# Attention scores and products with v in rounds of four 64x64 array quarters, with loads reordered and dense groups mixed

## Chip, cores, metric

One core of a Trainium2 chip runs the whole program. The metric is device time in microseconds (us) of one execution. A profile's span is about 1.8 us shorter than the time of the same execution.

## The reference

Batch 8, 12 heads, 448 tokens, head size 64, then a dense block on 3584 tokens:

```python
scores = (1.0 / np.sqrt(64)) * np.matmul(q, k.transpose(0, 1, 3, 2))
attn = np.maximum(scores, 0.0) ** 2 / 448
x = np.matmul(attn, v)              # heads merged: 3584 x 768
h = x @ w_in                        # 768 x 2048
r = np.maximum(h, 0.0)
out = (r * r) @ w_out               # 2048 x 768, float32
```

Attention is worked off in 24 *units* of four heads (three units a batch). The dense block is worked off in *groups*: an h group (6 matmuls, 128 rows of h for one batch) or an output group (16 matmuls, 128 tokens by 384 columns). Output groups need all 16 h groups of their batch. *g* is the squared relu of h that they read. In the profiles the tiles of h are called hps, those of the outputs ops, score tiles sp (their relu sr, their squares at), and the products with v avt, which are scaled into xt.

## The kernel before

Tokens of k are cut into three chunks of 128 and a tail of 64. q and k are cast to fp16 and transposed by DMA. ACT writes relu to SBUF as fp32, DVE multiplies it by itself. A queue holds the dense matmuls, and pieces of it are put between the attention work of a unit.

```python
s_p = ...tile_pool(name="sps", bufs=2, space=PSUM)     # 2 score buffers of 2 banks
mm_p = ...tile_pool(name="mmps", bufs=4, space=PSUM)   # 4 banks for all else

def relu2(ps, dst, shape, tag, scale):
    r = rel_p.tile(shape, FP32, name=tag, tag=tag)
    nc.scalar.activation(out=r, in_=ps, func=AF.Relu, scale=scale)
    nc.vector.tensor_mul(dst, r, r)

def scores(n, hp, t):              # two matmuls side by side, 64 rows each
    ...
    for j in range(2):
        r = slice(64 * j, 64 * j + 64)
        nc.tensor.matmul(sp[:, j, 0:S], lhsT=kT[r, 3 * hp + t, :], rhs=qT[r, hp, :], ...)
# ... scores_tail: four matmuls in the four 64x64 quarters; av: both forms ...

for n in range(NUN):
    # ... loads of unit n+3 ...
    g = [scores(n, 0, 0), scores(n, 0, 1)]; soft(...); soft(...)
    fill(...)                      # dense matmuls from the queue
    st = scores_tail(n)
    if n > 0:
        av(n - 1)                  # 4 + 12 matmuls, DVE scales the result into xt
    soft(n, "tail", st)
    if u == 0 and n > 0:
        push_h(b - 1)              # 16 h groups, then the output groups they allow
        # ... push_o(...) ...
    fill(...)
    # ... w1 loads at n == 0, w2 loads at n == 1, casts and DMA transposes of unit n+2 ...
    g = [scores(n, 0, 2), scores(n, 1, 0)]; soft(...); soft(...)
    fill(...)
    g = [scores(n, 1, 1), scores(n, 1, 2)]; soft(...); soft(...)
    fill(...)
```

Of the kernel before, what the change touches and what calls it, by code (L numbers as in the profile page):

```python
# [15 lines left out]
def kernel(  # L17
# [9 lines left out]
    nc = tc.nc  # L27
# [8 lines left out]
    QP = 112  # L36
    QJ = S // QP
    NU = 3
    NM = DM // P
    NF = FF // P  # L40
    HALF = DM // 2
    KM = 384
    ST = S - KM

# [7 lines left out]
    in_p = ctx.enter_context(tc.tile_pool(name="inp", bufs=2))  # L52
# [3 lines left out]
    rel_p = ctx.enter_context(tc.tile_pool(name="relp", bufs=2))  # L56
    at_p = ctx.enter_context(tc.tile_pool(name="atp", bufs=11))
    x_p = ctx.enter_context(tc.tile_pool(name="xp", bufs=2))
    g_p = ctx.enter_context(tc.tile_pool(name="gp", bufs=32))
    osb_p = ctx.enter_context(tc.tile_pool(name="osbp", bufs=2))  # L60
# [8 lines left out]

    raw: dict = {}  # L70
    qkt: dict = {}
    vst: dict = {}
    ktt: dict = {}

    def load_q(n, eng):
        b, u = divmod(n, NU)
        qf = raw_p.tile([QP, 4, QJ * D], FP32, name="qf", tag="qf")
        eng.dma_start(
            out=qf, in_=q[b, 4 * u:4 * u + 4].rearrange("h (p j) d -> p h (j d)", j=QJ))
        raw[n, "q"] = qf  # L80

    def load_k(n, eng):
        b, u = divmod(n, NU)
        kf = raw_p.tile([P, 4, 3 * D], FP32, name="kf", tag="kf")
        eng.dma_start(
            out=kf, in_=k[b, 4 * u:4 * u + 4, 0:KM].rearrange("h (p t) d -> p h (t d)", t=3))
        raw[n, "k"] = kf

    def turn_q(n, ops):
        qf = raw.pop((n, "q"))  # L90
        qs = blk_p.tile([QP, 2, QJ, 2 * D], FP16, name="qs", tag="qs")
        for j in range(2):
            ops[j](qs[:, :, :, j * D:(j + 1) * D],  # L93
                   qf.rearrange("p (a j) (t d) -> p a j t d", j=2, d=D)[:, :, j])
        qT = qkt_p.tile([P, 2, S], FP16, name="qT", tag="qT")
        nc.sync.dma_start_transpose(
            out=qT.rearrange("p a (j c) -> p (a j) c", j=QJ),
            in_=qs.rearrange("p a t d -> p (a t d)"))
        qkt[n, "q"] = qT

    def turn_k(n, ops):
        kf = raw.pop((n, "k"))
        ks = blk_p.tile([P, 2, 3, 2 * D], FP16, name="ks", tag="ks")
        for j in range(2):
            ops[j](ks[:, :, :, j * D:(j + 1) * D],  # L105
                   kf.rearrange("p (a j) (t d) -> p a j t d", j=2, d=D)[:, :, j])
        kT = qkt_p.tile([P, 6, P], FP16, name="kT", tag="kT")
        nc.sync.dma_start_transpose(  # L108
            out=kT, in_=ks.rearrange("p a t d -> p (a t d)"))
        qkt[n, "k"] = kT  # L110

    def load_kt(b):
        kt = in_p.tile([ST, H, D], FP16, name="kt", tag="kt")
        nc.gpsimd.dma_start(out=kt, in_=k[b, :, KM:S].rearrange("h p d -> p h d"))
        raw[b, "t"] = kt

    def turn_kt(b):
        kt = raw.pop((b, "t"))
        ktT = in_p.tile([P, NM, ST], FP16, name="ktT", tag="ktT")
        nc.sync.dma_start_transpose(out=ktT, in_=kt.rearrange("p h d -> p (h d)"))  # L120
        ktt[b] = ktT

    def load_v(b, h0, h1):
        if b not in vst:
            vst[b] = (in_p.tile([P, H, 3 * D], FP16, name="vs", tag="vs"),
                      in_p.tile([P, H, D], FP16, name="vt", tag="vt"))
        nc.gpsimd.dma_start(
            out=vst[b][0][:, h0:h1, :],
            in_=v[b, h0:h1, 0:KM].rearrange("h (p t) d -> p h (t d)", t=3))

    def load_vt(b):

        for r in range(2):
            nc.gpsimd.dma_start(
                out=vst[b][1][64 * r:64 * r + 64],
                in_=v[b, :, KM:S].rearrange("h p d -> p h d"))

    pool2 = (nc.gpsimd.tensor_copy, nc.gpsimd.tensor_copy)
    dve2 = (nc.vector.tensor_copy, nc.vector.tensor_copy)
    act2 = (nc.scalar.copy, nc.scalar.copy)  # L140
# [13 lines left out]

    load_q(0, nc.sync)
    load_k(0, nc.scalar)
    load_kt(0)
    load_q(1, nc.sync)
    load_k(1, nc.scalar)
    load_v(0, 0, 4)  # L160
    load_vt(0)
    load_w1(0)
    load_v(0, 4, H)
    turn_q(0, dve2)
    turn_k(0, act2)
    turn_kt(0)
    load_q(2, nc.sync)
    load_k(2, nc.sync)
    turn_q(1, dve2)
    turn_k(1, dve2)  # L170


# [5 lines left out]
    def push(cost, fn):  # L178
        nonlocal queued
        fifo.append((cost, fn))  # L180
        queued += cost

    def run_some(ns):
        nonlocal queued
        while fifo and ns > 0:
            c, fn = fifo.popleft()
            fn()
            queued -= c
            ns -= c
        return ns  # L190

    def relu2(ps, dst, shape, tag, scale):
        r = rel_p.tile(shape, FP32, name=tag, tag=tag)
        nc.scalar.activation(out=r, in_=ps, func=AF.Relu, scale=scale)  # L194
        nc.vector.tensor_mul(dst, r, r)  # L195

    def push_h(b):
# [7 lines left out]
        def step(f, m):  # L205
            def run():
# [6 lines left out]
                if m == NM - 1:  # L213
                    if b % 2 == 0:
                        gt[f] = g_p.tile([P, 2 * S], FP16, name="g", tag="g")
                    relu2(cell[0][:, 0:S], gt[f][:, (b % 2) * S:(b % 2 + 1) * S],
                          [P, S], "hr", 1.0)
            return run

        for f in range(NF):  # L220
            for m in range(NM):
                push(189.0, step(f, m))

    def store(pr, tb, osb):
        c = tb * P
        end = c + P
        while c < end:
            b = 2 * pr + c // S
            cb = c % S
            j, p0 = cb // QP, cb % QP  # L230
            n = min(QP - p0, end - c)
            r = c - tb * P
            nc.sync.dma_start(
                out=out[b * S:(b + 1) * S, :].rearrange(
                    "(p j) d -> p j d", j=QJ)[p0:p0 + n, j, :],
                in_=osb[r:r + n, :],
            )
            c += n

    def push_o(pr, tb):  # L240
# [21 lines left out]
        for hf in range(2):  # L262
            for f in range(NF):
                push(162.5, step(hf, f))
# [4 lines left out]
    def soft(n, key, sp):  # L269
        at = at_p.tile([P, 2, S], FP16, name="at", tag="at")  # L270
        relu2(sp[:, :, 0:S], at, [P, 2, S], "sr", SK)
        ats[n, key] = at

    def scores(n, hp, t):
        qT, kT = qkt[n, "q"], qkt[n, "k"]
        sp = s_p.tile([P, 2, 512], FP32, name="sp", tag="s")
        for j in range(2):
            r = slice(64 * j, 64 * j + 64)
            nc.tensor.matmul(  # L279
                sp[:, j, 0:S], lhsT=kT[r, 3 * hp + t, :],  # L280
                rhs=qT[r, hp, :], start=True, stop=True)
        return sp



    QUADS = ((0, 0, 0), (0, 1, 1), (1, 0, 1), (1, 1, 0))

    def scores_tail(n):
        b, u = divmod(n, NU)
        qT, kt = qkt[n, "q"], ktt[b]  # L290
        sp = s_p.tile([P, 2, 512], FP32, name="sp", tag="s")
        for hp, j, c in QUADS:
            r = slice(64 * j, 64 * j + 64)
            nc.tensor.matmul(  # L294
                sp[64 * c:64 * c + 64, hp, 0:S], lhsT=kt[r, 2 * u + hp, :],
                rhs=qT[r, hp, :], start=True, stop=True)
        return sp

    def av(n):
        b, u = divmod(n, NU)  # L300
        vs, vt = vst[b]
        ap = [mm_p.tile([P, 512], FP32, name="avt", tag="mm") for _ in range(2)]
        for hp, j, c in QUADS:
            r = slice(64 * c, 64 * c + 64)
            nc.tensor.matmul(  # L305
                ap[hp][64 * j:64 * j + 64, 0:S], lhsT=vt[r, 4 * u + 2 * hp + j, :],
                rhs=ats[n, "tail"][r, hp, :],
                start=True, stop=False, skip_group_check=True)
        for hp in range(2):
            for t in range(3):  # L310
                for j in range(2):
                    nc.tensor.matmul(  # L312
                        ap[hp][64 * j:64 * j + 64, 0:S],
                        lhsT=vs[:, 4 * u + 2 * hp + j, t * D:(t + 1) * D],
                        rhs=ats[n, (hp, t)][:, j, :],
                        start=False, stop=(t == 2), skip_group_check=True)
            nc.vector.tensor_scalar(  # L317
                out=xts[b][:, 2 * u + hp, :], in0=ap[hp][:, 0:S],
                scalar1=CX, scalar2=None, op0=ALU.mult)

    NUN = B * NU
    KEEP = 4000.0

    def fill(atoms_left):
        run_some(max(0.0, (queued - KEEP) / atoms_left))

    for n in range(NUN):
        b, u = divmod(n, NU)
        if n + 3 < NUN:
            load_q(n + 3, nc.sync)  # L330
            load_k(n + 3, nc.sync)
# [81 lines left out]
```

## Time and profile before

| | before |
|---|---|
| time, median of 7 runs | 467.2 us (466.2 to 468.6) |
| first score matmul / first dense matmul (hps) / first output matmul (ops) | 19.5 / 76.2 / 102.2 us |
| two batches in the steady part | 99.8 us |
| busy: PE / DVE / ACT | 389 / 300 / 236 us |

The page cuts the span (465.7 us) into 40 slices of 11.6 us; a digit is the busy share in tenths.

```profile
PE   0113157899999999989998999989998999999995
DVE  2152567996699367975787469955995478834500
DMA  9999999903891559706990469227933320021022
```

PE (TensorE) is nearly full from the ninth slice on, and at 0 to 5 tenths in the first six, where the DMA row stands at 9. So there are two regimes: a start of some 75 us held by DMA (loads and DMA transposes), and a long part held by TensorE. The chain of work that ended last says what the start waited for; its columns are start us, us, what. It is cut to the start.

```profile
7.25 12.15 DMA kT<-ks
...
26.71 20.22 DMA qf<-in_q_dram
...
53.52 10.71 DMA kf<-in_k_dram
...
70.09 2.78 DMA ktT<-kt
```

Each of the four long pieces is a DMA: the transpose of unit 0's k takes 12.15 us among the loads of weights, a load of q takes 20.22 us. What PE waited for kT, the transposed k, over the whole span (us in total, times, longest):

```profile
PE sp L279 <- DMA kT<-ks: 45.2, 3, 19.5
```

Here is how the first looks in the timeline of PE (start us, us, engine, line, operation, tiles, count, and in brackets the idle time and its releaser):

```profile
302.66 0.65 PE L248 MATMUL ops<-w_3_100,g 128*128 128x384 f16 x3
304.96 0.34 PE L248 MATMUL ops<-w_3_100,g 128*128 128x384 f16 x1 [1.64 <-DVE g L195]
```

Last, the time of DVE's two products, as min/median/max in ns:

```profile
L195 DVE TENSOR_TENSOR at<-sr x168: 1075/1085/2957, 21.0 to 415.0; 128x896 f16<-128x896 f32 x168
L195 DVE TENSOR_TENSOR g<-hr x128: 609/624/1926, 78.9 to 440.5; 128x448 f16<-128x448 f32 x128
```

The medians are 1.2 and 1.4 ns for each element of a partition.

### The profile page before, as it was taken

The numbers are of one execution on the slowest core, as the hardware profiler recorded it, in microseconds if no ns is written. First come the engines' busy times: TensorE is split into PE (matmuls) and PEld (weight loads), VectorE is DVE, ScalarE is ACT, GpSimd is POOL, SyncE is SP. The second block draws the span as 40 slices with busy tenths as digits, with TensorE's granted clock in tenths as the row PEclk, the third lists the DMA queues.
The fourth block names the chain that finished last, engine by engine and source line by source line (L and its number), as shares of the span: only waits on it lengthen the run. The fifth ranks groups of instructions, "written<-read, shape, count | busy, mean of one in ns | idle before, by whom it ended". The sixth has DMA issues, their size and how long they took to land.

```text
span 465.7 us, 6359 instructions
## 1 busy us (share of the span) xinstructions
PE 388.9 (84%) x2432; PEld 185.2 (40%) x2432; DVE 299.7 (64%) x350; ACT 236.4 (51%) x355; POOL 108.2 (23%) x133
## 2 busy tenths in 40 slices
PE   0113157899999999989998999989998999999995
PEld 0001013444444444444444544444444444455563
DVE  2152567996699367975787469955995478834500
ACT  1232354575565457556565456735654567543421
POOL 6050528510442005500432043402440000000000
PEclk9999656999999999999999999999999999999999
DMA  9999999903891559706990469227933320021022
GB/s 208 199 216 218 206 225 220 211 2 80 159 240 39 81 140 175 157 1 156 156 207 1 114 152 220 65 63 163 203 91 71 90 59 1 1 68 35 0 69 68
DMA packets 109614, 56.25 MB, mean 121 GB/s; under 512 B 77840, under 2 KB 106000, under 8 KB 109584
## 3 DMA queue, kind: packets, MB, share of 16 engines
q1 hardware_dynamic: 72032, 41.69, 40.2%
q0 software_dynamic: 36496, 13.37, 24.6%
q10 hardware_dynamic: 1056, 0.79, 0.6%
q8 instruction: 19, 0.31, 0.3%
q14 instruction: 11, 0.09, 0.1%
HBM read 47.19 MB, written 11.01 MB: 125 GB/s over the span
## 4 chain that ended last, share of the span: by engine, by line
PE 51%; DVE 24%; DMA 11%; ACT 8%; SPq 2%; issue 2%; POOL 1%; ACTq 0%; POOLq 0%
PE ops L248 29%; DVE at L195 15%; PE hps L209 12%; DVE g L195 8%; ACT sr L194 6%; DMA qf<-in_q_dram 5%; PE avt L312 5%; PE sp L279 4%; DMA kT<-ks 3%; DMA kf<-in_k_dram 2%; ACT hr L194 2%; SPq L108 1%; PE sp L294 1%; DVE xt L317 1%; PE avt L305 1%
## 5 line engine op out<-in xcount | busy, mean ns | idle before, releaser
L195 DVE TENSOR_TENSOR at<-sr 128x896 f16<-128x896 f32 x168 | 186.7, 1147 | 102.0 <-ACT sr L194 101.5
L194 ACT ACTIVATE sr<-sp 128x896 f32<-128x896 f32 x168 | 147.0, 918 | 91.3 <-PE sp L279 75.8
L248 PEld LDWEIGHTS <-g 128*128 128x128 f16 x896 | 84.0, 98 | 77.6 <-issue 13.9
L194 ACT ACTIVATE hr<-hps 128x448 f32<-128x448 f32 x128 | 68.5, 553 | 60.3 <-DVE g L195 31.9
L195 DVE TENSOR_TENSOR g<-hr 128x448 f16<-128x448 f32 x128 | 89.8, 731 | 13.8 <-ACT hr L194 12.1
L93 POOL CAST qs<-qf 112x512 f16<-112x512 f32 x44 | 41.0, 958 | 231.3 <-DMA qf<-in_q_dram 229.7
L279 PE MATMUL sp<-qT,kT 64*128 64x448 f16 x288 | 44.1, 377 | 52.8 <-DMA kT<-ks 45.2
L255 ACT ACTIVATE osb<-ops 128x384 f32<-128x384 f32 x56 | 27.5, 492 | 69.0 <-PE ops L248 68.9
L248 PE MATMUL ops<-w_3_100,g 128*128 128x384 f16 x224 | 47.7, 327 | 8.6 <-DVE g L195 8.6
L248 PE MATMUL ops<-w_0_97,g 128*128 128x384 f16 x224 | 47.1, 326 | 0.0
L248 PE MATMUL ops<-w_2_99,g 128*128 128x384 f16 x224 | 46.4, 327 | 0.0
L248 PE MATMUL ops<-w_1_98,g 128*128 128x384 f16 x224 | 46.3, 326 | 0.0
L279 PEld LDWEIGHTS <-kT 64*128 64x128 f16 x288 | 9.4, 95 | 81.2 <-DMA kT<-ks 46.4
L317 DVE TENSOR_SCALAR xt<-avt 128x448 f16<-128x448 f32 x48 | 28.2, 618 | 18.9 <-PE avt L312 18.9
L209 PE MATMUL hps<-xt,w_3_96 128*128 128x448 f16 x192 | 40.0, 353 | 0.0
L209 PE MATMUL hps<-xt,w_0_93 128*128 128x448 f16 x192 | 39.6, 358 | 0.0
L209 PE MATMUL hps<-xt,w_1_94 128*128 128x448 f16 x192 | 39.5, 353 | 0.0
L209 PE MATMUL hps<-xt,w_2_95 128*128 128x448 f16 x192 | 39.0, 353 | 0.5 <-ACT hr L194 0.5
L105 POOL CAST ks<-kf 128x384 f16<-128x384 f32 x44 | 34.9, 819 | 2.9 <-DMA kf<-in_k_dram 1.7
L312 PE MATMUL avt<-at,vs 128*64 128x448 f16 x288 | 35.2, 385 | 0.0
L209 PEld LDWEIGHTS <-w_0_93 128*128 128x128 f16 x192 | 18.4, 99 | 19.6 <-issue 4.2
L209 PEld LDWEIGHTS <-w_2_95 128*128 128x128 f16 x192 | 18.2, 98 | 19.5 <-issue 3.3
(26 smaller groups left out, 116.0 us busy)
## 6 DMA issues: line engine op xcount, KB each, us to landing
qf<-in_q_dram SPq DMA_DIRECT2D x24, 448.0 KB, 5.8
kf<-in_k_dram SPq DMA_DIRECT2D x22, 384.0 KB, 6.7
vs<-in_v_dram POOLq DMA_DIRECT2D x7, 576.0 KB, 7.6
out_dram<-osb SPq DMA_DIRECT2D x8, 336.0 KB, 3.0
out_dram<-osb SPq DMA_DIRECT2D x8, 288.0 KB, 2.8
out_dram<-osb SPq DMA_DIRECT2D x8, 240.0 KB, 3.0
vt<-in_v_dram POOLq DMA_DIRECT2D x16, 96.0 KB, 8.2
out_dram<-osb SPq DMA_DIRECT2D x8, 192.0 KB, 2.7
```

The source lines that it names most:

```text
L93: ops[j](qs[:, :, :, j * D:(j + 1) * D], qf.rearrange("p (a j) (t d) -> p a j t d", j=2, d=D)[:, :, j])
L105: ops[j](ks[:, :, :, j * D:(j + 1) * D], kf.rearrange("p (a j) (t d) -> p a j t d", j=2, d=D)[:, :, j])
L108: nc.sync.dma_start_transpose(out=kT, in_=ks.rearrange("p a t d -> p (a t d)"))
L194: nc.scalar.activation(out=r, in_=ps, func=AF.Relu, scale=scale)
L195: nc.vector.tensor_mul(dst, r, r)
L209: nc.tensor.matmul(cell[0][:, 0:S], lhsT=w1[f // 4][:, m, (f % 4) * P:(f % 4 + 1) * P], rhs=xt[:, m, :], start=(m == 0), stop=(m == NM - 1))
L248: nc.tensor.matmul(cell[0][:, 0:HALF], lhsT=gt[f][:, tb * P:(tb + 1) * P], rhs=w2[f // 4][:, f % 4, hf * HALF:(hf + 1) * HALF], start=(f = ...
L255: nc.scalar.activation(out=cell[1][:, hf * HALF:(hf + 1) * HALF], in_=cell[0][:, 0:HALF], func=AF.Copy, scale=CO)
L279: nc.tensor.matmul(sp[:, j, 0:S], lhsT=kT[r, 3 * hp + t, :], rhs=qT[r, hp, :], start=True, stop=True)
L294: nc.tensor.matmul(sp[64 * c:64 * c + 64, hp, 0:S], lhsT=kt[r, 2 * u + hp, :], rhs=qT[r, hp, :], start=True, stop=True)
L312: nc.tensor.matmul(ap[hp][64 * j:64 * j + 64, 0:S], lhsT=vs[:, 4 * u + 2 * hp + j, t * D:(t + 1) * D], rhs=ats[n, (hp, t)][:, j, :], start ...
L317: nc.vector.tensor_scalar(out=xts[b][:, 2 * u + hp, :], in0=ap[hp][:, 0:S], scalar1=CX, scalar2=None, op0=ALU.mult)
```

## The change

The intent: use all four 64x64 quarters in every round of attention, so that there is one kind of round, seven per unit, without a tail; load k whole; get the first units going early by loading q, k, v of the first units ahead of the weights and transposing units 0 to 5 on PE; even out the work by taking always two rounds (a *burst*) between pieces of dense work, by mixing h and output groups, and by moving work between ACT and DVE. Core of the diff, cuts marked:

```diff
+    def load_qk(n, w, gate=None):          # q and k alike, 1792 bytes a row
+        t = raw_p.tile([P, 2, TJ * D], FP32, name=w + "f", tag=w + "f")
+        if gate is not None:
+            gate.memset(t[:, 0, 0:1], 0.0)     # holds the load back until DVE is there
 ...
+    def turn_pe(n, w, op):                 # units 0 to 5; later ones by DMA
+        for t in range(TJ):
+            nc.tensor.transpose(ps[:, t * P:(t + 1) * P], src[:, t, :], ident)
+        op(t.rearrange("p t c -> p (t c)"), ps)
 ...
-    def relu2(ps, dst, shape, tag, scale):
-        r = rel_p.tile(shape, FP32, name=tag, tag=tag)
-        nc.scalar.activation(out=r, in_=ps, func=AF.Relu, scale=scale)
-        nc.vector.tensor_mul(dst, r, r)
+    def relu2(ps, dst, scale):
+        nc.scalar.activation(out=dst, in_=ps, func=AF.Square, scale=scale)
+        nc.vector.scalar_tensor_tensor(
+            out=dst, in0=ps, scalar=0.0, in1=dst, op0=ALU.is_gt, op1=ALU.mult)
 ...
+    def push_dense(b):
+        hs = h_groups(b)
+        if b % 2 == 1:
+            os_ = [g for tb in range(3) for g in o_groups(b // 2, tb)]
+        elif b > 0:
+            os_ = [g for tb in range(3, 7) for g in o_groups(b // 2 - 1, tb)]
+        else:
+            os_ = []
+        # ... os_ spread evenly between the 16 h groups; the last outputs at the end ...
 ...
+    def scores(n, t):
+        for e in range(2):
+            for f in range(2):
+                c = f ^ e
+                r = slice(64 * f, 64 * f + 64)
+                nc.tensor.matmul(sp[64 * c:64 * c + 64, e, 0:S]..., lhsT=kT[r, t, 64 * e:64 * e + 64],
+                    rhs=qT[r, :, 64 * e:64 * e + 64], start=True, stop=True)
 ...  (av: seven such rounds, 28 matmuls)
-            nc.vector.tensor_scalar(out=xts[b][:, 2 * u + hp, :], in0=ap[hp][:, 0:S], scalar1=CX, ...)
+            nc.scalar.activation(out=xts[b][:, 2 * u + f, :], in_=ap[f][:, 0:S], func=AF.Copy, scale=CX)
 ...
+    for i in range(NB):                    # 84 bursts
+        g = []
+        for r in (2 * i, 2 * i + 1):
+            n, t = divmod(r, TJ)
+            g.append((n, t, scores(n, t)))
+        if i in avs:
+            av(avs[i])
+        for a in g:
+            soft(*a)
+        if i in pushes:
+            push_dense(pushes[i])
+        upkeep(i)                          # loads, casts, transposes; w1 at unit 0, w2 at unit 3
+        nxt = min([j for j in pushes if j > i] or [NB + 2])
+        run_some(max(0.0, (queued - KEEP) / (nxt - i)))
```

The output groups that batch b makes possible are no longer queued behind its own h groups but among those of batch b+1. I call this the deferral.

## The prediction

> **What bounds it now.** The page's first six slices of 40 (to 73 us) show PE at 0 to 5 tenths, DMA at 9. The chain there: loads and kT transposes by DMA: the first score matmul starts at 19.45 us, unit 1 at 42.2 (16.1 us waited for kT), unit 2 at 60.3 (9.7 waited), the first dense matmul (hps) at 76.2. From about 95 us TensorE bounds: the stretches show it busy 47.5 of 50 us. Two batches take 99.8 us (chain: 152.9, 252.7, 352.9).
>
> **PE work does not shrink.** Dense matmuls pitch at 189 ns (96 in 18.16 us) and 162.7 ns (128 in 20.82 us): 290 us in all. Attention is 14 rounds a unit before and after, about 0.19 us each, as the four-quarter tail rounds show: 63 us stay too.
>
> **What changes.**
> 1. Start: transposes of units 0 to 5 move from DMA to PE; q, k of units 0 to 2 and v load ahead of w1, w2 later. First scores at about 10 us. Units 0 to 2 are then paced by two score buffers, now held through ACT (0.92 us) and DVE (about 1.1), plus 0.55 us for matmul and hand-offs: 1.3 us a round. 24 rounds plus copies: dense starts near 48 us. The next ten bursts hold only h(0), bound by DVE: 20 x 1.1 + 16 x 0.65 us and copies, about 38 us. So 22 bursts and h(0) are done near 86 us; before finished h(0) at 104. w2, all needed for the first output group, should land near 78 us at the 300 GB/s of source bytes estimated from w2's loads before.
> 2. DVE: at<-sr (1085 ns median) and g<-hr (624) become one op with a PSUM operand. The Trainium skill (VectorE: DVE Perf Modes, "Why PSUM operands drop a tier") puts fp32 from PSUM at 1x; the old op already shows that pace, so no gain per op. xt (48 x 0.6 us) goes to ACT: DVE falls from 300 to 265 us, ACT rises from 236 to 275, both off the critical path later.
> 3. Putting scores between dense work costs about 0.21 us beyond their rounds (161.69 to 162.44: 0.54 of work took 0.75). The Trainium skill (TensorEngine Tiling (Array Packing), "Key Properties") says changing the tiling mode drains the engine; the trace agrees. 84 replace 96 insertions: about 4 us saved.
> 4. Against: score buffers free only after DVE, and ACT does xt first after each product with v. I estimate 0.6 to 1 us of PE wait per unit; the pair period falls to about 98. One third of an output block moves into the tail: 55 us instead of 40, no work added.
>
> **Sum.** 86 us at burst 22; 3 x 47 + 3 x 51.5 us for six batches; 55 tail; 5 to finish: about 441. I take 438, 6% faster, nearly all from the start.
>
> **Signs.** First scores near 10, first hps at 42 to 55, PE at 9 tenths from 85 to 90; DVE ops of 1.05 to 1.15 and 0.6 to 0.7 us; pair period 95 to 100; pure dense at the end 50 to 57; no DMA transposes in the first 60 us.
>
> **What would make it wrong.** w2 landing after 90 us; four weight loads a round not hiding (rounds of 0.22 us, +10 us); PE waiting for score buffers every burst (+20 to 40); or mixing groups removing more waits than I think (420).

## More of the kernel before

For the rest of the kernel, the waits of PE between 150 and 350 us (four batches). Columns: engine, group, who released it, us in total, times, longest.

```profile
PE ops L248 <- DVE g L195: 6.3, 4, 1.6
PE sp L294 <- ACT sr L194: 3.3, 4, 0.8
PE sp L279 <- ACT sr L194: 0.2, 1, 0.2
```

The first output matmul waits for the last g out of DVE, about 1.6 us a batch, and the tail scores wait for a score buffer.

## The result

| | before | after |
|---|---|---|
| time, median of 4 runs each | 466.87 us | 444.25 us (442.76 to 446.55) |
| ratio | | 0.9525 (95% interval 0.9465 to 0.9585) |
| first score / hps / ops matmul in the profile | 19.5 / 76.2 / 102.2 us | 8.3 / 56.0 / 101.0 us |
| two batches in the steady part | 99.8 us | 95.5 us |
| dense work alone at the end | about 40 us | 59 us |
| busy: PE / DVE / ACT | 389 / 300 / 236 us | 397 / 250 / 262 us |

Ratios here and below are the mean time of one kernel's runs over that of the other's of the same rounds, so they are not quite the ratio of the medians quoted. The kernel became 4.75% faster, where 6% was predicted; 444.25 us is 6 us above the predicted 438.

The page's slices after (11.0 us each):

```profile
PE   2565687799999999999999999999999999999995
DVE  2754577776766574676586566486657555222100
DMA  9699899667335764494647462595461111111122
```

PE is at 5 to 8 tenths where it was at 0 to 5, and full from the ninth slice (88 us). But busy is not work done. To see where time was won I counted PE's matmuls by their start and weighed each at its pitch, the time from start to start in an unbroken row (189 ns for h, 162.5 ns for output, 187.5 ns for a round of attention); the whole program is about 354 us of such work in both kernels. Up to 100 us, before had done 88 h matmuls and 61 rounds, 28.1 us of work; after, 109 h matmuls and 92 rounds, 37.9 us. So at 100 us the lead is 9.8 us, although the first output matmul starts at about the same time. At 360 us the lead is 20.0 us (278.6 against 258.6), and the spans end 24.7 us apart. **The start gave less than half of the gain; the steady part gave about as much.** That is not how the prediction split it.

What the start waits for now is the score buffers. These are the instructions around the first product with v (PE, ACT, DVE out of the timeline after):

```profile
23.65 0.59 PE L240 MATMUL sp<-qT,kT 64*64 64x448 f16 x4 [0.41 <-DVE at L151]
23.97 2.88 PE L263 MATMUL avt<-at,vs 64*64 64x448 f16 x28
26.91 0.98 ACT L269 ACTIVATE xt<-avt 128x448 f16<-128x448 f32 x2 [4.44 <-PE avt L263]
27.77 1.74 ACT L150 ACTIVATE at<-sp 128x896 f16<-128x896 f32 x2
28.73 2.09 DVE L151 SCALAR_TENSOR_TENSOR at<-sp,at 128x896 f16<-128x896 f32 x2 [5.13 <-ACT at L150]
29.87 0.38 PE L240 MATMUL sp<-qT,kT 64*64 64x448 f16 x4 [1.50 <-DVE at L151]
```

Read from the top: PE does the second round of the burst at 23.65 and goes on with the 28 matmuls of the product with v. ACT is free, and the scores are there, but in ACT's program order the xt copies come first, so it idles 4.44 us until the product is done. Only then come the two squares, then DVE (idle 5.13 us), and only when DVE has read a score buffer may PE start the next scores, at 29.87. From first round to first round this burst takes 7.2 us (22.65 to 29.87); an ordinary burst takes 2.73 us (19.92 to 22.65).

The wait of PE for score buffers after, over the whole span (us in total, times, longest):

```profile
PE sp L240 <- DVE at L151: 30.7, 39, 3.0
```

And the same line, of the same kernel, for 150 to 350 us alone:

```profile
PE sp L240 <- DVE at L151: 3.0, 6, 0.5
```

In the steady part PE waits 3.0 us in 200 us instead of 9.8 (the three lines of before). That is 1.4 us per two batches instead of 4.9, which is 3.5 of the 4.3 us by which two batches became shorter.

The DVE operations after:

```profile
L151 DVE SCALAR_TENSOR_TENSOR at<-sp,at x168: 1080/1082/1093, 9.9 to 370.1; 128x896 f16<-128x896 f32 x168
L151 DVE SCALAR_TENSOR_TENSOR g<-hps,g x128: 614/616/626, 59.5 to 413.3; 128x448 f16<-128x448 f32 x128
```

The medians hardly moved, the long ones are gone: 1093 ns is the longest of 168, where it was 2957. The means fell from 1147 to 1086 and from 731 to 618 ns. POOL's casts became regular too: 929 to 943 ns for 896 elements, where 512 elements took 603 to 1567 ns before. The Trainium skill (SBUF — State Buffer, "Who interferes with whom") explains it: a DVE instruction with two SBUF inputs takes its second input through a read interface that GpSimd's reads use too; one with at most one SBUF input, outside the two-port modes, does not contend. The traces agree: the old product read SBUF twice, the new one reads PSUM and SBUF, and when e5 brought the old product back, both its times (up to 1818 ns) and those of POOL's casts (929 to 3753 ns for the same 896 elements) spread again.

### The profile page after: what moved, and what is told of

Read it like the earlier page. It is cut to its first block, busy times and chain, and to the rows that moved or that the text cites. A ratio compares the mean times of both kernels' runs of the same rounds, so it can differ in the third digit from the quotient of the medians.

```text
span 441.0 us, 7546 instructions
## 1 busy us (share of the span) xinstructions
PE 396.6 (90%) x3092; PEld 202.9 (46%) x3092; DVE 250.3 (57%) x309; ACT 261.8 (59%) x408; POOL 69.6 (16%) x92
## 4 chain that ended last, share of the span: by engine, by line
PE 76%; DVE 9%; ACT 8%; issue 4%; DMA 1%; SPq 0%; ACTq 0%; DVEq 0%
PE ops L194 31%; PE hps L166 27%; PE sp L240 9%; DVE at L151 9%; PE avt L263 8%; ACT at L150 4%; ACT xt L269 3%; PE tps L103 1%; DMA kf<-in_k_dram 1%; ACT kT L105 0%; DVE g L151 0%; DVE qT L105 0%; ACT ks L89 0%; ACT osb L201 0%; SPq L80 0%
## 5 line engine op out<-in xcount | busy, mean ns | idle before, releaser
L151 DVE SCALAR_TENSOR_TENSOR at<-sp,at 128x896 f16<-128x896 f32 x168 | 175.3, 1086 | 117.5 <-ACT at L150 117.3
L150 ACT ACTIVATE at<-sp 128x896 f16<-128x896 f32 x168 | 147.2, 925 | 27.9 <-PE sp L240 24.3
L151 DVE SCALAR_TENSOR_TENSOR g<-hps,g 128x448 f16<-128x448 f32 x128 | 76.6, 618 | 41.0 <-ACT g L150 40.8
L240 PE MATMUL sp<-qT,kT 64*64 64x448 f16 x672 | 58.9, 392 | 34.0 <-DVE at L151 30.7
L150 ACT ACTIVATE g<-hps 128x448 f16<-128x448 f32 x128 | 68.9, 560 | 29.0 <-PE hps L166 28.5
L269 ACT ACTIVATE xt<-avt 128x448 f16<-128x448 f32 x48 | 23.5, 541 | 58.0 <-PE avt L263 58.0
L89 POOL CAST qs<-qf 128x896 f16<-128x896 f32 x23 | 21.5, 935 | 152.5 <-DMA qf<-in_q_dram 133.7
L263 PE MATMUL avt<-at,vs 64*64 64x448 f16 x672 | 39.7, 375 | 0.0
L114 POOL DMA_DIRECT2D vs<-in_v_dram x32 | 20.1, 636 | 94.8 <-PE hps L166 74.9
L263 PEld LDWEIGHTS <-vs 64*64 64x64 f16 x672 | 22.5, 114 | 12.5 <-issue 0.4
```

What stands on the lines that cost most here:

```text
L89: op(t.rearrange("p t (f d) -> p f t d", f=2), src.rearrange("p f (t d) -> p f t d", d=D))
L114: nc.gpsimd.dma_start(out=vst[b][64 * r:64 * r + 64, :, e, :], in_=src[h])
L150: nc.scalar.activation(out=dst, in_=ps, func=AF.Square, scale=scale)
L151: nc.vector.scalar_tensor_tensor(out=dst, in0=ps, scalar=0.0, in1=dst, op0=ALU.is_gt, op1=ALU.mult)
L240: nc.tensor.matmul(sp[64 * c:64 * c + 64, e, 0:S].rearrange("p (t c) -> p t c", t=TJ), lhsT=kT[r, t, 64 * e:64 * e + 64], rhs=qT[r, :, 64 ...
L263: nc.tensor.matmul(ap[f][64 * e:64 * e + 64, 0:S], lhsT=vs[r, u, e, t * D:(t + 1) * D], rhs=at[r, e, :], start=(t == 0), stop=(t == TJ - 1 ...
```

## The experiments

All were correct on the chip. The kernel before, run beside each, had medians of 467.4, 466.8, 466.7 and 467.2 us. "Pair" is the time of two batches, from the start of one product with v in the chain to that two batches later.

| run | what was done | time us | ratio to before | hps / ops first | pair us |
|---|---|---|---|---|---|
| e1 | nothing (control) | 446.9 | 0.955 | 59.9 / 106.1 | – |
| e2 | units 2 to 5 transposed by DMA | 449.5 | 0.962 | 54.3 / 107.8 | – |
| e3 | w1 loaded first | 445.0 | 0.953 | 57.3 / 104.2 | – |
| e4 | squares ahead of xt on ACT | 428.4 | 0.917 | 52.5 / 92.1 | 93.45 |
| e5 | relu through fp32 again | 433.4 | 0.928 | 52.9 / 96.8 | 93.45 |
| e6 | dense groups not mixed | 447.1 | 0.957 | 59.8 / 125.9 | 96.2 |
| e7 | xt on DVE again | 432.7 | 0.928 | 53.9 / 96.3 | 93.45 |
| e8 | before, weights later | 458.5 | 0.983 | 69.6 / 92.9 | 99.6 |
| e9 | not deferred | 436.6 | 0.935 | 59.5 / 84.3 | 96.1 |
| e10 | e4 and fp16 relu | 421.9 | 0.905 | 41.9 / 85.8 | 93.4 |
| e11 | e5 and e9 | 436.0 | 0.934 | 52.2 / 78.1 | 96.7 |
| e12 | e10 and e9 | 410.5 | 0.878 | 40.2 / 64.3 | 93.45 |

### e1: the control

> The changed kernel again, unedited, as the yardstick for the runs of this call. Every theory: 442 to 447 us, first scores near 8.3 us, first dense matmul near 56 us, two batches of the steady part in 95.5 us.

Median 446.94 us (442.52 to 448.19): the median is just inside what I wrote, two of the four runs are above it, and the profile's first scores (11.2 us) and first dense matmul (59.9 us) are late. The profiled run (span 446.1 us) suggests why the eight times of this kernel fall in two clusters (442.5 to 442.9 and 445.6 to 448.2 us): the cast of unit 0's k, which waits for its load, started at 8.3 us instead of 5.4, and everything after followed. There is only one profile from each cluster, so this is likely and not shown. The profiles of e6, e9 and e10 had the same late load (7.9 to 8.5 us). So differences of 4 to 5 us between two profiles of the start mean nothing, and medians are to be preferred. Below, gains are counted from the 444.25 us of the result; from this control they would be 2.7 us larger.

### e2: DMA transposes for units 2 to 5

```diff
-    NPE = 6
+    NPE = 2
```

> Undoes one part: only units 0 and 1 are transposed on PE, units 2 to 5 by DMA as before. Theory A (a good part of the gain at the start is DMA transposes that no longer queue behind loads): unit 2 to 5 wait for kT by 3 to 15 us in all, first dense matmul at 60 us or later, total 447 to 457 us. Rival B (the start is now paced by the round trip scores, ACT, DVE, scores; DMA transposes would have been hidden): first dense matmul within 2 us of 56, total within 3 us of the control, or a little faster as 8 x 7 transposes leave PE.

449.51 us (448.75 to 450.08), inside A's range, but rival B's signs hold as well: the first dense matmul did not come later (54.3 us), and the median is within 3 us of the control's. PE waited 5.3 us for kT, as A said, and the first output matmul came at 107.8 us. The profile after, with the same early load of k, ended 6.8 us sooner; against the control, whose runs mix both clusters, it is 2.6 us by medians, and the two intervals of the ratio overlap. So these 56 transposes on PE are worth perhaps 3 to 7 us, at the later units, not at the first dense matmul; the runs do not settle it.

### e3: w1 first

```diff
     load_v(0, (2, 3))
+    for z in range(4):
+        load_w1(z)
 ...
-                    for z in range(4):
-                        load_w1(z)
```

> Undoes one part: all of w1 is issued at about 5 us, right behind v of batch 0, instead of after the casts of unit 2 (15.6 us). Theory A (loading q and k ahead of the weights matters): q and k of units 1 and 2 land later by 3 to 10 us, unit 1 or 2 waits on PE, first dense matmul 59 to 66 us, total 446 to 454 us. Rival B (q and k are on another queue and keep their share): first dense matmul within 2 us of 56, total within 2 us of the control.

444.99 us, first dense matmul 57.3 us: rival B. With PE transposing, holding w1 back behind q and k of the first three units gives nothing.

### e4: squares ahead of xt

```diff
-        if i in avs:
-            av(avs[i])
         for a in g:
             soft(*a)
+        if i in avs:
+            av(avs[i])
```

> One edit: in a burst with the product with v, ACT's squares of the two score tiles are put ahead of its two xt copies. In the trace of the changed kernel ACT stood idle 4.0 to 4.4 us for av in each of the first three such bursts and the next scores came 5.8 to 7.2 us after the last ones instead of 2.7. Theory A (ACT held by xt costs the start 3 to 4 us in each of three bursts and 1 us later): first dense matmul 46 to 50 us, total 428 to 437 us. Rival B (PE's in-order queue is the limit: the scores of the next burst stand behind the 28 matmuls anyway, 2.9 us cold): first dense matmul 53 to 57 us, total 439 to 444 us.

428.42 us (427.26 to 429.46): theory A's total. The same place in the timeline:

```profile
23.10 1.92 ACT L150 ACTIVATE at<-sp 128x896 f16<-128x896 f32 x2 [0.81 <-PE sp L240]
23.47 0.59 PE L240 MATMUL sp<-qT,kT 64*64 64x448 f16 x4 [0.41 <-DVE at L151]
23.79 2.87 PE L263 MATMUL avt<-at,vs 64*64 64x448 f16 x28
24.05 2.09 DVE L151 SCALAR_TENSOR_TENSOR at<-sp,at 128x896 f16<-128x896 f32 x2 [0.64 <-ACT at L150]
26.72 0.98 ACT L269 ACTIVATE xt<-avt 128x448 f16<-128x448 f32 x2 [1.70 <-PE avt L263]
28.20 0.64 PE L240 MATMUL sp<-qT,kT 64*64 64x448 f16 x8
```

ACT and DVE do the squares while PE does the product with v, and at 28.20 both score buffers are free (8 matmuls in one go, where after managed four at 29.87). What now precedes them on PE is its own work, 28 matmuls and 14 transposes. The bursts with the first two products took 5.7 and 4.1 us where after took 7.2 and 6.8. The first dense matmul came at 52.5 us, though, and not at 46 to 50 as A said: with the buffers free the cold product of 2.9 us and the transposes remain ("cold" is this slow state: at 52 us of the changed kernel the 28 matmuls took 2.88 us at a granted clock of 0.50, at 171 us they took 1.49 us at 1.00. But at 24 us they took the same 2.88 us while the records give 1.00, so at the start the clock record does not show the slow state), so that rival B's limit exists as well. The gain is spread: 3.5 us at the first dense matmul, 9 us at the first output matmul, and the wait between 150 and 350 us is gone altogether; two batches take 93.45 us. That is close to the work itself (84 rounds, 192 h and 224 output matmuls: 88.4 us) plus 21 insertions (places where rounds of attention stand between dense matmuls) at 0.22 us, 4.6 us.

### e5: relu through fp32 again

```diff
-        nc.scalar.activation(out=dst, in_=ps, func=AF.Square, scale=scale)
-        nc.vector.scalar_tensor_tensor(out=dst, in0=ps, scalar=0.0, in1=dst, ...)
+        nc.scalar.activation(out=r, in_=ps, func=AF.Relu, scale=scale)   # r: fp32 in SBUF
+        nc.vector.tensor_mul(dst, r, r)
```

> Undoes one part: ACT writes relu as fp32 to SBUF and DVE multiplies it by itself, as before the change; score buffers are free after ACT again. Theory A (the fused op from PSUM, which no longer shares SBUF reads with POOL's casts, is what shortens the steady part): DVE ops spread up to 2 us again, mean of at 1.12 to 1.16 us, two batches take 98 to 100 us instead of 95.5, total 448 to 456 us. Rival B (mixing h and output groups does it, DVE has slack): DVE ops spread, but two batches stay within 1 us of 95.5. At the start every theory: pairs of rounds in 2.2 to 2.5 us instead of 2.73, first dense matmul 3 to 6 us earlier, so under B the total is 436 to 441 us.

433.36 us, 11 us faster than the changed kernel.

```profile
L153 DVE TENSOR_TENSOR at<-sr x168: 1074/1086/1818, 10.5 to 360.8; 128x896 f16<-128x896 f32 x168
```

Theory A fell: DVE's operations spread again (1818 ns at most, mean 1176), and yet two batches took 93.45 us. Rival B had the direction, but the size surprised both: the fused operation costs about 11 us in this kernel, because it keeps the score buffer through ACT *and* DVE: PE's wait for score buffers over the whole span fell from 30.7 us (for DVE) to 17.3 (for ACT). The steady part was helped by undoing it, not hurt.

### e6: groups not mixed

```diff
-            upto = (i + 1) * len(os_) // len(hs)
+            upto = len(os_) if i == len(hs) - 1 else 0
```

> Undoes one part: the 16 h groups of a batch are queued first and its output groups after them, as before. Theory B (mixing evens the load of ACT and DVE and so takes the waits out of the steady part): two batches in 97.5 to 100 us, total 447 to 455 us. Theory A (the fused op does it): two batches within 1 us of 95.5, total within 3 us of the changed kernel's 444.

447.14 us, pair 96.2: no more than 0.7 us from 95.5, and 0.2 us from the control's median. Mixing as such does nothing here. The total alone would fit theory B's range too, but its pair time did not come: theory B fell, and A fell with e5, so the steady gain needed a third explanation (e9, e11).

### e7: xt on DVE again

```diff
-            nc.scalar.activation(out=xts[b][:, 2 * u + f, :], in_=ap[f][:, 0:S], func=AF.Copy, scale=CX)
+            nc.vector.tensor_scalar(out=xts[b][:, 2 * u + f, :], in0=ap[f][:, 0:S], scalar1=CX, ...)
```

> Undoes one part: xt is scaled out of PSUM by DVE, as before, instead of by ACT. If ACT held by xt is what costs the start (A): ACT goes on with the squares at once but DVE stands behind xt, so the score buffers come free no sooner; gain 0 to 5 us, total 439 to 445. If the place of xt does not matter (B): within 2 us of 444.

432.71 us: a gain of 12 us, more than either theory allowed. In the trace the squares now run under the product with v; behind it stand two xt (1.16 us) and one fused operation (1.08 us) before the first buffer is free, where after had two xt, one square and one fused operation (0.98, 0.9 and 1.08 us). That is about 0.7 us less at each product, and PE's waits between 150 and 350 us are zero in this run; that the one is enough for the other is my reading.

### e8: before, with the weights later

```diff
-    load_w1(0)
 ...
-        if n == 0: (w1, 1 to 3)
-        if n == 1: (w2)
+        if n == 1: (w1)
+        if n == 3: (w2)
```

> The kernel before with one part of the change alone: w1 is loaded two units later and w2 behind unit 3, so q, k and v of the first units have the DMA engines to themselves; transposes stay on DMA. Theory A (load order is a large part of the start): waits for kT at units 1 and 2 (16.1 and 9.7 us) fall to 0 to 4 us, first dense matmul 50 to 62 us instead of 76, total 450 to 460 us. Rival B (the transposes by DMA are slow by themselves): the waits stay above 8 us in all and the total within 5 us of 467.

458.50 us, 8 us better. Units 1 and 2 no longer wait (their scores start at 23.8 and 34.5 us instead of 42.2 and 60.3), as A said. But the waits came back one unit later, at unit 3:

```profile
47.89 0.93 PE L278 MATMUL sp<-qT,kT 64*128 64x448 f16 x4 [4.35 <-DMA kT<-ks]
66.31 0.59 PE L293 MATMUL sp<-qT,ktT 64*64 64x448 f16 x4 [17.49 <-DMA ktT<-kt]
```

PE waits 4.35 us for kT and then 17.49 us for the transposed tail of the second batch's k, so that the first dense matmul is at 69.6 us, not at 50 to 62. So in the kernel before, later weights are worth about 8 us (ratio 0.983, 95% interval 0.980 to 0.985: clear of noise, but classed "unclear" on record, because it does not clear the 2% that counts as faster there). This is no share of the 22 us: in the changed kernel e3 found that the place of w1 is worth nothing. That the load order would be worth more without DMA transposes and the tail of k is not shown.

### e9: output groups behind their own h groups

```diff
-        if b % 2 == 1:
-            os_ = ... o_groups(b // 2, tb) for tb in range(3)
-        elif b > 0:
-            os_ = ... o_groups(b // 2 - 1, tb) for tb in range(3, 7)
+        tbs = range(3) if b % 2 == 0 else range(3, 7)
+        os_ = [g for tb in tbs for g in o_groups(b // 2, tb)]
 ...
-            upto = (i + 1) * len(os_) // len(hs)
+            upto = len(os_) if i == len(hs) - 1 else 0
```

This undoes the mixing as well, which e6 showed to be worth nothing by itself.

> Undoes one part of the changed kernel: the output groups that a batch makes possible are queued right behind its own h groups, as before, instead of with the next batch's h groups. Theory A (the deferral, not the mixing, took the wait of the first output matmul for the last g out of the steady part): the wait ops for DVE g of about 1.6 us comes back in each of the batches 1 to 7 (6 to 13 us in all, 5 to 7 us between 150 and 350 us), two batches take 98 to 99.5 us instead of 95.5. But dense work is there earlier, so PE is fuller between 60 and 100 us; total 440 to 452 us. Rival B (the deferral does not matter): no wait of ops for g, two batches within 1 us of 95.5, total 438 to 447 us.

436.63 us: 8 us faster than the changed kernel, and below both ranges. The wait of ops for g stayed small, 0.8 us between 150 and 350 us, so A's wait did not come back, and two batches took 96.1 us. The gain is the earlier dense work. At 60 us this kernel had done 9.2 us of work (its profile has the late load of k), at 100 us 44.7 us; the changed kernel had 11.5 and 37.9.

### e10: e4 and fp16 relu

```diff
     (e4's edit)
-        nc.scalar.activation(out=dst, in_=ps, func=AF.Square, scale=scale)
-        nc.vector.scalar_tensor_tensor(out=dst, in0=ps, scalar=0.0, in1=dst, ...)
+        nc.scalar.activation(out=dst, in_=ps, func=AF.Relu, scale=scale)
+        nc.vector.tensor_mul(dst, dst, dst)
```

> The squares ahead of xt, as in the 428 us kernel, and ACT writing relu as fp16 which DVE then squares fp16 by fp16 in place: score buffers are free after ACT, and the DVE op has 16-bit operands only. Theory A (the start is paced by the round trip through both engines): DVE op of 0.5 to 0.65 us on 896 elements, pairs of rounds at the start in 2.0 to 2.3 us instead of 2.73, first dense matmul 44 to 49 us instead of 52.5, total 419 to 425 us. Rival B (after the reordering the start is held by loads and by PE's cold clock): first dense matmul 50 to 53 us, total 425 to 430 us. In the steady part every theory: two batches within 0.5 us of 93.4. Should stay correct: one more fp16 rounding.

421.90 us, first dense matmul at 41.9 us although k had landed late. The score buffer is free after ACT, bursts at the start take 1.6 us (A said 2.0 to 2.3), and the DVE operation has a median of 626 ns for 896 elements instead of 1082:

```profile
L151 DVE TENSOR_TENSOR at<-at x168: 611/626/1344, 12.5 to 349.1; 128x896 f16<-128x896 f16 x168
```

The Trainium skill (VectorE: DVE Perf Modes, "The perf-mode tier table") puts `tensor_tensor` on bf16 operands in SBUF at 2x, on fp32 at 1x; the trace, with fp16, agrees in the main: 626 ns against the 1086 of e5's fp32 product, 1.7 times as fast. Single ones took up to 1344 ns, while POOL's casts took 923 to 1390. Theory A, with its first dense matmul even earlier than it said. New waits appeared, 6.2 us for a kT by DMA and 1.4 us for v: the start is now near its loads.

### e11: e5 and e9 together

The edit is that of e5 and that of e9:

```diff
+        nc.scalar.activation(out=r, in_=ps, func=AF.Relu, scale=scale)   # r: fp32 in SBUF
+        nc.vector.tensor_mul(dst, r, r)
 ...
+        os_ = [g for tb in tbs for g in o_groups(b // 2, tb)]    # behind the h groups of b
```

> Both undone: relu through fp32 in SBUF, multiplied by DVE, and the output groups queued right behind their own h groups. The kernel before waited 6.3 us (four times, up to 1.6 us) between 150 and 350 us for the last g ahead of the first output matmul; either alone had no such wait or 0.8 us. Theory A (each of the two changes is enough to take this wait away: the fused op keeps DVE's queue short, the deferral makes the g old): the wait comes back with 3 to 7 us between 150 and 350 us, two batches take 95 to 98 us. Rival B (neither: the even bursts of two rounds or xt on ACT took it away): under 1.5 us there, two batches in 93.4 to 94.5 us. Total, with dense work there earlier: A 427 to 434 us, B 422 to 428 us.

436.03 us, pair 96.7. The wait of PE for the last g between 150 and 350 us in e9:

```profile
PE ops L194 <- DVE g L151: 0.8, 2, 0.4
```

The lines of e11 for the same stretch:

```profile
PE ops L195 <- DVE g L153: 4.7, 2, 2.4
PE sp L237 <- ACT sr L152: 0.5, 2, 0.3
```

With both undone, 4.7 us of the wait for the last g are back, in two long pieces; with only the deferral undone it was 0.8 us, with only the fused operation undone (e5) none. The wait and the pair time are theory A's; the total is 2 us above its range. So either of the two takes most of this wait away, and the change had both. But this is the smaller part of the steady gain: with both undone two batches still take 3.1 us less than the 99.8 of before, out of 4.3. The wait for score buffers (0.5 us here, 3.5 before) and three insertions fewer (0.7 us a pair) are what is left, and neither needs the fused operation or the deferral.

### e12: e10 and e9 together

The edit is that of e10 and that of e9:

```diff
         for a in g:
             soft(*a)
+        if i in avs:
+            av(avs[i])
 ...
+        nc.scalar.activation(out=dst, in_=ps, func=AF.Relu, scale=scale)   # dst: fp16
+        nc.vector.tensor_mul(dst, dst, dst)
 ...
+        os_ = [g for tb in tbs for g in o_groups(b // 2, tb)]    # behind the h groups of b
```

> The fastest kernel so far (421.9 us: squares ahead of xt, fp16 relu squared by DVE) with the output groups of a batch right behind its own h groups, which in the changed kernel alone took 444 to 436.6 us. Theory A (PE lacks dense work between 42 and 60 us): PE fills earlier by 3 to 6 us, total 415 to 419 us. Rival B (there the kernel is held by loads: w2 lands too late for an output group that comes at about 60 us, and kT of unit 6 was waited for 6.2 us): PE waits for w2 or kT by as much as it gains, total 419 to 425 us.

410.52 us (410.40 to 410.72), ratio 0.878 to before: the fastest version, 7.6% faster than the changed kernel by medians, better than A said. Neither kT nor w2 was waited for. Its slices are 10.2 us each:

```profile
PE   2767999999999999999999999999999999999995
DVE  1756474346523455236523365326532355203200
DMA  8599999698245962497136983486326600120032
```

PE is full from the fifth slice, 41 us. Between 60 and 80 us it does 18.5 us of work, where e10 did 11.3: there e10 had only the thinly spread h groups of batch 0, and it stood 6.2 us for the kT of unit 6. This run fills the same time with output groups and comes to that kT later, without waiting; how much of its 11 us over e10 is which was not told apart.

## Why the prediction was right, and where it was not

1. **PE's work does not shrink: right.** Both kernels hold about 354 us of it, and rounds of four quarters pitch at 0.19 us also seven in a row: after, 9 rounds (scores and product with v) and both mode changes fill 170.79 to 172.71 us, 1.92 us. Four weight loads a round were hidden. The layout that gives the change its name saved TensorE nothing by itself.
2. **"First scores at about 10 us": right** (8.3). "1.3 us a round": right (2.73 us per two).
3. **"24 rounds plus copies: dense starts near 48 us": too early, 56.0.** The first dense matmul follows the product of unit 2, which comes in the thirteenth burst (50.9 us), so 26 rounds go before it, not 24: 2.7 us. Products, transposes and copies added 12.2 us to the 13 bursts, where the prediction had left 6.8 (48 less 10 and 24 x 1.3). The term that was too small is "0.6 to 1 us of PE wait per unit" at the product with v. ACT idled 4.0 to 4.4 us in each of the first three, and the bursts with the first two took 7.2 and 6.8 us instead of 2.73. Of this, e4 gives the order on ACT 1.5 and 2.7 us (3.5 up to the first dense matmul, 8.9 up to the first output matmul); the rest is PE's own 28 matmuls and 14 transposes. I had named the order ("ACT does xt first") and spread its cost evenly. Over the whole kernel e4 gained 16 us by medians (18.5 against the control), 0.7 to 0.8 us a unit, as forecast on average; but more than half of it falls in the first 100 us.
4. **"22 bursts and h(0) are done near 86 us": the 23rd burst starts at 89.2, h(0) ends at 97.** So by work done the start is 10 us ahead of before and not 18, and "nearly all from the start" is wrong.
5. **"The pair period falls to about 98": it fell to 95.5.** I allowed for 0.21 us per insertion (measured: 0.22), but here the same term was too large: 0.6 to 1 us a unit is 3.6 to 6 us a pair, and after loses 1.4. Before lost 4.9 us a pair waiting for the last g and for score buffers, which I had not counted as a gain. e11, e9 and e5 show that the fused operation or the deferral suffices against the first. The second is 0.5 us or less between 150 and 350 us in e5, e7 and e11, so neither the fused operation nor xt on ACT nor the deferral removed it. That the even bursts did is argued by elimination only: no run undid them alone. The two errors, in 3 and 5, nearly cancelled by luck, which is how 438 came so close to 444.
6. **"No gain per op" on DVE: right for the medians, wrong for the means**, as POOL no longer stretches them. DVE fell to 250 us, not 265. It did not matter to the time, as e5 shows: the fused operation lost more by keeping score buffers than DVE won.
7. **The tail: 59 us rather than 55,** probably since the schedule keeps 4 us of dense work in hand. **w2 landed at about 69.5 us** (issued at 47.4, 22.1 us to landing), before it was needed, so that risk did not come true. The risk "PE waiting for score buffers every burst" came true at the start only.

What stays open: the share of single parts of the new start (whole k instead of a tail, transposes of units 0 and 1 on PE, v's place) was not told apart. e8 puts later weights at 8 us in the kernel before, e3 puts the place of w1 at nothing in the changed one, and e2 the later transposes at perhaps 3 to 7.

## What to carry to other kernels

When an accumulator buffer is read by two engines in turn, it is held for the sum of both and for whatever stands before them in program order: put the instructions that free a scarce buffer ahead of those that wait for later matmuls. Undo each part of a bundled change once it has won: here three parts that looked like improvements (the fused operation, xt on ACT, the deferral) each cost 8 to 12 us inside a change that gained 22 (the costs do not add up: undoing the first and the third together gave 436.0 us, no more than the third alone). A part that is harmless where TensorE has work in stock can be the limit where it has none, so size a term in the stage in which it acts.

## What the Trainium skill lacked or had wrong

- TensorEngine Tiling (Array Packing), "Key Properties", says that changing the tiling mode drains the engine, but gives no cost. Here one insertion of 64x64 rounds between 128x128 matmuls, two changes, cost 0.22 us (the next h matmul was due at 161.78 us by the pitch and began at 162.38: 0.60 us for 0.38 us of rounds).
- TensorE: Matmul & The Clock Gate, "Part 4: PE-mode transpose", gives about 275 ns for a 128x128 transpose in a kernel, and no pitch. Single ones took 219 to 315 ns here, which agrees, but back to back they overlap: 14 took 1.62 us in the chain at 43.5 us, at a granted clock of 0.50 (116 ns each), and a set of 7 began 0.40 us after the one before it at 71 us, at 1.00 (57 ns each).
- SBUF — State Buffer, "Who interferes with whom", was right and I did not use it: the product with two SBUF inputs took up to 2957 ns beside POOL's casts (median 1085), the one with one input at most 1093. It gives no size for how much the mean suffers; here 6% (1147 against 1086) and 18% (731 against 618).
- No page says that a load's landing at the start can differ between executions of one program: in the two profiles of the changed kernel the cast of unit 0's k began at 5.4 and at 8.3 us, and the spans were 441.0 and 446.1 us (over all its versions: 5.1 to 6.0 us in eight profiles, 7.9 to 8.5 in four).
